# An attention step that begins with a pair of scores and maxima, and orders the two halves of its background by a one-column read

## The chip, the core and the metric

The kernel runs on one core of a Trainium2 chip. The metric is the device time of one execution in microseconds; lower is better.

The engines of the core, with the names that the profile gives them: TensorE (PE, matmuls; PEld, the loading of a matmul's weights, which overlaps the matmul before), VectorE (DVE), ScalarE (ACT), GpSimd (POOL), and the queue that issues DMAs (SP). Matmul results go to eight banks of PSUM, each 128 x 512 numbers of 32 bits.

## The reference

A transformer block with a conditioning vector: layer norm, attention with 32 heads of 16 dimensions over 2048 tokens of width 512, and a feed-forward part of width 1792.

```python
mod = (silu(c) @ w_mod).reshape(1, 6, 1, 512)
sa, ca, ga, sb, cb, gb = (mod[:, i] for i in range(6))
h = layernorm(x) * (1 + ca) + sa
q, k, v = heads(h @ wqkv)                       # 32 heads, 16 dimensions each
p = softmax(q @ k.T * 16 ** -0.5)               # 2048 x 2048 for each head
x = x + ga * ((p @ v) @ wo)
h = layernorm(x) * (1 + cb) + sb
x = x + gb * (gelu(h @ w1 + b1) @ w2 + b2)
```

## The kernel before

After a prologue of some 110 us the kernel walks through attention in 512 **steps** (`half_step(hs)`, `for hs in range(NU * NKC)`): 32 units of one block of 512 queries and a group of four heads, times 16 blocks of 128 keys. All else that TensorE has to do (projections, output projection, both feed-forward products) is put between the attention matmuls as **background**. At the end a tail of some 120 us does the last block's feed-forward part.

Four kinds of matmul stand in a step:

- `mx` (`mx_mm`, L387): scores of a unit that comes later, only to find their maxima. VectorE reduces each to one column, negated (`reduce`, L392). The maxima are sent through DRAM into two more rows of the queries, so that the scores of the unit come out with their maximum taken off.
- `e` (`exp_mm`, L637): the scores themselves. ScalarE turns each into a tile `p` by an exponential (L642).
- `bg` (`bg_mm`, through `mm`, L274): background.
- `pv` (`pv_step`, L667): four matmuls with `p`, one for each head of the group, at the step's end.

`e`, `mx` and `bg` use only 64 rows of the array (50, 48 and 64 of them), so two run at once, one in each **half** of the rows. A step of number `hs` has half `h = hs % 2`: six background matmuls go to half `h`, and `e` and `mx` beside them to the other half, `1 - h`. Two matmuls beside each other are called a **pair** here. A step has seven: six with background and one of an `e` in half `h` and an `mx` in half `1 - h`. So each step has four `e`, four `mx`, six `bg` and the four `pv`; with the background of two steps both halves of the rows have added to the result.

A group of background (12 or 18 terms for each half) takes four or six steps, and all its matmuls add to one bank. At its end ScalarE, by `evac`, copies the bank out (`y` L834 and L906, `h` L880, `pf` L308, `vr` L322).

Matmuls of the two halves that add to one bank may not run at once. So where a group goes on in the other half, its first matmul there waits for an instruction of ScalarE that can only be done after the last matmul of the half before: `saw` notes the first such instruction after each background matmul, and `bg_mm` adds the dependency.

```python
        if g["n"] and g["half"] != h:
            tc.add_manual_dep(ins, g["seen"].name, AFTER, reason="both halves of the rows add to one bank")
        g["half"], g["seen"] = h, None
```

Banks go round in rings: three for `e` (0, 1, 2), three for `mx` (3, 4, 5), one for `pv` (6), one for `bg` (7). A matmul into a bank waits until the bank's last reader is done, so the fourth `e` of a step waits for the exponential of the first, and an `mx` for the reduction of the third `mx` before it. Each engine works off its instructions in the order in which the program writes them.

Some steps differ: 12 in which `turn_v` first transposes values on TensorE and ScalarE copies them (`vst`, L338), 12 that begin with the transposes of a layer norm's result (`h`, L853), 13 in which no background is ready, and the last 22, for which no maxima are left. ScalarE also does the Tanh of the feed-forward part (`s`, L886), copies weights (`wqkv`, L190) and takes each unit's result out of its bank (`osb`, L654). VectorE finds each unit's minimum of the negated maxima (`mn`, L404), transposes it (`mt`, L406), and does statistics of rows (`bst`, `mv`, `rt`) and reciprocals (`dn`).

Of the kernel before, what the change touches and what calls it, by code (L numbers as in the profile page):

```python
# [8 lines left out]
F32 = mybir.dt.float32  # L9
FR = mybir.dt.float32r  # L10
AF = mybir.ActivationFunctionType
# [5 lines left out]
P = 128  # L17
# [42 lines left out]
RUN = 6  # L60
# [9 lines left out]
def block_kernel(ctx: ExitStack, tc: tile.TileContext, x, wqkv, wo, w1, b1, w2, b2, c, w_mod, out):  # L70
    nc = tc.nc
    te, ve, ac, gp, sy = nc.tensor, nc.vector, nc.scalar, nc.gpsimd, nc.sync
# [13 lines left out]
    def bank(i, name):  # L86
        return bank_pools[i].tile([P, TB], F32, tag=f"bank{i}", name=name)
# [6 lines left out]
    def take(name):  # L94
        ids = rings[name]
        turn[name] += 1
        return bank(ids[(turn[name] - 1) % len(ids)], name)
# [13 lines left out]
    const = ctx.enter_context(tc.tile_pool(name="const", bufs=1))  # L111
# [12 lines left out]
    gb_b = const.tile([P, D], F32, name="gb_b")  # L124
    b2_b = const.tile([P, D], F32, name="b2_b")
    b1_h = const.tile([P, NF], F32, name="b1_h")


    kqcm, kqpool = pool("kq")
# [27 lines left out]
    first = [True]  # L157
# [109 lines left out]
    def advance():  # L267
        clock["t"] += 1
        for f in hooks.pop(clock["t"], []):
            f()  # L270
# [82 lines left out]
    def kh(u, h):  # L353
        return khalf[(2 * u + h) % 5]

    def load_rows(dst, w, g, t0, t1):

        ap = qk_d[w][g // 2].rearrange("i d (g p a) t -> g a (i d) p t", g=2, p=2)
        for a in range(2):
            sy.dma_start(dst[a * 64 : a * 64 + KR].bitcast(F32), ap[g % 2, a, :, :, t0:t1])  # L360
# [5 lines left out]
    def load_q(u):  # L366
# [2 lines left out]
        qst[u] = kqpool.tile([P, 2, TB], FR, tag="qst", name="qst", bufs=3)  # L369
        load_rows(qst[u], 0, g, qb * TB, (qb + 1) * TB)  # L370

    xc, red, mrows = [0, 0], {}, set()
    xorder = [int(t[1]) for t in SCRIPT.split() if t[:2] in ("X0", "X1") for _ in range(int(t[3:] or 1))]
    xorder = [(u, xorder[:n].count(u)) for n, u in enumerate(xorder)]
# [2 lines left out]
    def mx_mm(a):  # L377

        u, i = xorder[xc[a]] if xc[a] < 64 else divmod(xc[a], 32)
        xc[a] += 1  # L380
        kr, p, qc = i // 8, (i // 4) % 2, i % 4
        if u not in mxp:
            mxp[u] = small.tile([P, 16, 4], F32, tag="mxp", name="mxp")
            red[u] = 0
        ps = take("mx")
        r0 = a * 64
        te.matmul(ps, qst[u][r0 : r0 + KR, p, qc * P : (qc + 1) * P],  # L387
                  kh(u, kr // 2)[r0 : r0 + KR, p, (kr % 2) * TB : (kr % 2 + 1) * TB], start=True, stop=True)
        hc = (a * 2 + p) * 4 + qc

        def reduce():
            ins = ve.tensor_reduce(mxp[u][:, hc, kr : kr + 1], ps, axis=AX.X, op=ALU.max, negate=True)  # L392
            red[u] += 1
            if red[u] == 64:
                max_rows(u)
            return ins

        return reduce
# [3 lines left out]
    def max_rows(u):  # L402
        m = mn[u % 2]
        ve.tensor_reduce(m[:, :16], mxp.pop(u), axis=AX.X, op=ALU.min)  # L404
        mt = small.tile([P, 32], F32, tag="mt", name="mt")
        ve.transpose(mt, m)  # L406
        m2 = small.tile([P, 2, 32], FR, tag="m2", name="m2")
        gp.tensor_copy(m2[:, 0], mt)
        gp.tensor_tensor(m2[:, 1], mt, m2[:, 0].bitcast(F32), op=ALU.subtract)

        def store():
            for i in range(2):
                sy.dma_start(m_d[u][i].rearrange("x b j -> b x j"), m2[:, i].bitcast(F32))

        def load():
            mrows.add(u)
            for a in range(2):
                r0 = a * 64 + KR
                sy.dma_start(qst[u][r0 : r0 + 2].bitcast(F32).rearrange("s p t -> s (p t)"),
                             m_d[u][:, a * 8 : a * 8 + 8].rearrange("s x b j -> s (x b j)"))  # L420

        if u:
            later(5, store)
            later(11, load)
        else:
            rows.update(store=store, load=load)
# [142 lines left out]
    for token in SCRIPT.split():  # L569
        name, ids, e, n = re.fullmatch(r"([A-Za-z]+)(\d*)(?:\.([avg]))?(?:\*(\d+))?", token).groups()  # L570
# [52 lines left out]
    ec, begun = [0, 0], [0]  # L623
    cur = {"pv": 0}

    def exp_mm(a, bk="e"):

        s, p = divmod(ec[a], 2)
        while begun[0] < min(ec) // 2 + 1:
            begun[0] += 1  # L630
            step_start(begun[0] - 1)
        ec[a] += 1
        u, kc = divmod(s, NKC)
        assert u in mrows, (u, ec, xc, red, clock["t"])
        r0 = a * 64
        ps = take(bk)
        te.matmul(ps, kh(u, kc // 8)[r0 : r0 + KX, p, (kc % 8) * P : (kc % 8 + 1) * P], qst[u][r0 : r0 + KX, p],  # L637
                  start=True, stop=True)

        def act():  # L640
            t = ppool.tile([P, TB], F32, tag="p", name="p")
            saw(ac.activation(t, ps, AF.Exp, scale=SCALE))  # L642
            pt[4 * s + p * 2 + a] = t
            advance()

        return act
# [122 lines left out]
    def wload():  # L769

        n = len(wt)
        if n == len(stream) or "f" not in pools:
            return
        key = stream[n]
        if extra:
            t = extra.pop()
        elif len(ringed) < WB or ringed[-WB] in used:
            t = pools["f"].tile([P, 2, D], FR, tag="w", name=f"w{key[1]}", bufs=WB)
            ringed.append(key)
        else:  # L780
            return
        sy.dma_start(t.bitcast(F32), {"o": wo_d, 1: w1_d, 2: w2_d}[key[1]][key[2]])
        wt[key] = t
# [198 lines left out]
    act = {"g": None}  # L982

    def saw(ins):

        if act["g"] and not act["g"]["seen"]:
            act["g"]["seen"] = ins.ins
# [23 lines left out]
    def half_step(hs):  # L1011
        h = hs % 2
        if h or len(wt) < len(used) + KC:
            wload()
        if sides:
            sides.pop(0)()
        full = False
        if act["g"] is None:
            j = held.pop() if held else next(jobs, None)
            if callable(j):  # L1020
                j()
                full = True
                j = next(jobs, None)
            if callable(j):
                held.append(j)
            elif j is not None:
                act["g"] = {"group": j, "at": [0, 0], "n": 0, "seen": None}
        nx = min(64 * NU, LEAD + 4 * (hs + 1))
        ne = 4 * (hs + 1)

        def x_ok(a):
            return sum(xc) < nx and xc[a] < 32 * NU

        def e_ok(a):
            return sum(ec) < ne and ec[a] < 2 * NU * NKC

        more = act["g"] is not None
        free = not more and not full
        k = 0
        while more and k < RUN:  # L1040
            a = 1 - h
            more = bg_mm(h)
            if e_ok(a) and (sum(ec) < ne - 1 and k % 2 == 1 or not x_ok(a) and (sum(ec) < ne - 1 or k == RUN - 1)):
                exp_mm(a)()
            elif x_ok(a):
                mx_mm(a)()
            k += 1
        while sum(ec) < ne or sum(xc) < nx:
            a = 0 if ec[0] <= ec[1] else 1
            fs = []  # L1050
            if sum(ec) < ne:
                fs.append(exp_mm(a, "bg" if free and sum(ec) == ne - 1 else "e"))
                if x_ok(1 - a):
                    fs.append(mx_mm(1 - a))
                elif e_ok(1 - a):
                    fs.append(exp_mm(1 - a))
            else:
                fs += [mx_mm(i) for i in range(2) if x_ok(i)]
            for f in fs:
                f()  # L1060
        if hs:
            assert min(ec) >= 2 * cur["pv"] + 2
            pv_step()
# [5 lines left out]
    def step_start(s):  # L1069
        u, kc = divmod(s, NKC)  # L1070
        for d in [d for d in due if d[0] <= s and all(k in stored for k in d[1])]:
            due.remove(d)
            d[2]()
        if kc == 0 and u + 2 < NU:
            g = (u + 2) % NG // 2
            due.append((16 * u + 6, [(0, g, (u + 2) // NG)], lambda: load_q(u + 2)))
            for b, n in enumerate((6, 8, 12, 13)):
                t0 = b % 2 * TB
                due.append((16 * u + n, [(1, g, b)], lambda b=b, t0=t0: load_k(u + 2, b // 2, t0, t0 + TB)))
        if kc == 0 and u + 1 < NU:  # L1080
            for h in range(2):
                need = [(2, (u + 1) % NG // 2, b) for b in (2 * h, 2 * h + 1)]
                due.append((16 * u + 11 + h, need, lambda h=h: load_v(u + 1, h)))
        if preps and s % 3 == 2:
            prep(*preps.pop(0))
        try_prep()

    for hs in range(NU * NKC):
        half_step(hs)
# [137 lines left out]
```

## Time and profile before

| what | value |
|---|---|
| median of three runs | 1730.08 us (1729.0 to 1730.61) |
| the profiled execution, first to last instruction | 1728.4 us |
| TensorE, matmuls | 1699.9 us busy, 98% of the span |
| VectorE | 1375.0 us, 80% |
| ScalarE | 1246.1 us, 72% |
| GpSimd | 694.7 us, 40% |
| mean granted TensorE clock | 0.999 of full speed |

The page gives the profiled execution no time of its own beside its span, which stands 1.7 us below the median. A row of a timeline gives start, length, engine, line, operation, output and inputs, and in brackets how long the engine was idle before and what ended that. Rows that follow each other and are alike are joined (x4). A row of a group has the busy time, the mean length of one in ns, and the idle time before. A row of the waits has who waited, for whom, us in total, times, and the longest. A row of a window has its bounds, its length, and busy time and count of PE and PEld; the last three numbers are the granted clock, the DMA engines' busy share and GB/s.

### The profile page before, as it was taken

To read this page: it belongs to the slowest core of one execution; us is meant where nothing else is said; L and a number is where in the kernel's file an instruction comes from. 1 tells how busy PE (TensorE), PEld (TensorE's weight loads), DVE (VectorE), ACT (ScalarE), POOL (GpSimd) and SP (SyncE) were. 2 spreads that over 40 slices of the span, in tenths; PEclk is the share of its full clock that TensorE was granted. 3 is DMA by queue.
4 is the path that set the end of the run, shared out by engine and by line. 5 is a ranking of instruction groups with operands and counts; after the bars stand their busy time and mean duration, and the time that the engine had idled before them with its cause. 6 is when DMAs were issued, how large, how long until landed. Compare 5 with 4: busy or idle time off the path is not lost.

```text
span 1728.4 us, 32510 instructions
## 1 busy us (share of the span) xinstructions
PE 1699.9 (98%) x12133; PEld 890.7 (52%) x12133; DVE 1375.0 (80%) x2307; ACT 1246.1 (72%) x2379; POOL 694.7 (40%) x703
## 2 busy tenths in 40 slices
PE   7999999999999999999999999999999999999999
PEld 5654444444444444444445444444445444444777
DVE  7998888888888888888889888888889888860332
ACT  3357778778777788778877788778877788778231
POOL 7333534435121457306623246306633256326310
PEclk9999999999999999999999999999999999999999
DMA  8746776767447534325453443345463354423444
GB/s 291 219 137 199 220 219 183 236 180 221 125 139 209 126 98 114 94 77 154 116 161 94 125 119 108 94 107 154 108 179 79 109 133 112 106 80 99 184 158 164
DMA packets 137129, 251.89 MB, mean 146 GB/s; under 512 B 25854, under 2 KB 45324, under 8 KB 136972
## 3 DMA queue, kind: packets, MB, share of 16 engines
q1 hardware_dynamic: 135712, 248.19, 50.3%
q8 instruction: 96, 1.57, 0.4%
q10 hardware_dynamic: 1260, 1.63, 0.3%
q14 instruction: 61, 0.50, 0.1%
HBM read 188.49 MB, written 61.28 MB: 145 GB/s over the span
## 4 chain that ended last, share of the span: by engine, by line
PE 91%; DVE 3%; DMA 2%; ACT 2%; POOL 1%; issue 1%; SPq 0%; ACTq 0%; DVEq 0%; POOLq 0%
PE bg L274 46%; PE pv L667 29%; PE e L637 11%; PE mx L387 3%; DVE mxp L392 2%; PE pr L274 1%; ACT p L642 1%; PE o L274 1%; DMA wm<-in_w_mod_dram 0%; DMA wt<-wos 0%; ACT h L853 0%; PE mx L333 0%; PE bg L851 0%; DMA rden<-dn 0%; DVE bst L235 0%
## 5 line engine op out<-in xcount | busy, mean ns | idle before, releaser
L392 DVE TENSOR_REDUCE mxp<-mx 128x1 f32<-128x512 f32 x2048 | 1269.6, 681 | 192.8 <-PE mx L387 160.6
L642 ACT ACTIVATE p<-e 128x512 f32<-128x512 f32 x2035 | 1072.9, 604 | 296.7 <-PE e L637 285.7
L387 PE MATMUL mx<-kh,qst 48*128 48x512 f32 x2048 | 865.3, 436 | 1.4 <-DVE mxp L392 0.3
L637 PE MATMUL e<-qst,kh 50*128 50x512 f32 x2035 | 747.6, 414 | 6.6 <-ACT p L642 6.4
L667 PE MATMUL pv<-p,vg 128*32 128x512 f32 x4096 | 546.1, 605 | 0.0
L637 PEld LDWEIGHTS e<-qst,kh 50*128 50x128 f32 x2035 | 374.2, 186 | 135.7 <-ACT p L642 128.5
L387 PEld LDWEIGHTS mx<-kh,qst 48*128 48x128 f32 x2048 | 369.0, 185 | 21.6 <-DVE mxp L392 14.9
L274 PE MATMUL bg<-w,g 64*128 64x512 f32 (+1 forms) x1056 | 280.6, 404 | 0.0
L274 PEld LDWEIGHTS bg<-w,g 64*128 64x128 f32 (+1 forms) x1056 | 185.3, 185 | 142.7 <-ACT p L642 83.9
L274 PE MATMUL bg<-pchi,w 64*128 64x512 f32 (+1 forms) x664 | 197.5, 417 | 2.3 <-ACT p L642 2.2
L274 PEld LDWEIGHTS bg<-pchi,w 64*128 64x128 f32 (+1 forms) x664 | 110.1, 184 | 153.2 <-ACT p L642 103.3
L274 PE MATMUL bg<-hThi,wqkv 64*128 64x512 f32 x560 | 167.4, 418 | 0.3 <-ACT p L642 0.3
L274 PEld LDWEIGHTS bg<-hThi,wqkv 64*128 64x128 f32 x560 | 92.8, 184 | 118.8 <-ACT p L642 106.3
L667 PEld LDWEIGHTS pv<-p,vg 128*32 128x32 f32 x4096 | 81.2, 108 | 124.6 <-issue 120.5
L888 POOL TENSOR_SCALAR s<-s 128x512 f32<-128x512 f32 x41 | 61.4, 1498 | 120.5 <-ACT s L886 120.5
L907 POOL TENSOR_TENSOR x<-y,x 128x512 f32<-128x512 f32 x28 | 36.0, 1287 | 153.5 <-ACT y L906 153.5
L274 PE MATMUL bg<-pclo,w 64*128 64x512 f32 (+1 forms) x332 | 90.1, 390 | 0.0
L876 DVE TENSOR_TENSOR g<-h,g 128x512 fp32r<-128x512 f32 x15 | 10.9, 725 | 88.1 <-ACT g L875 88.1
L274 PE MATMUL bg<-hTlo,wqkv 64*128 64x512 f32 x280 | 76.4, 391 | 0.0
L274 PEld LDWEIGHTS bg<-pclo,w 64*128 64x128 f32 (+1 forms) x332 | 61.2, 184 | 12.2
L274 PE MATMUL bg<-wo,pchi 64*128 64x512 f32 x192 | 64.6, 416 | 0.0
L881 POOL TENSOR_TENSOR s<-h 128x512 f32<-128x512 f32 x41 | 42.7, 1042 | 47.7 <-ACT h L880 47.6
(158 smaller groups left out, 1299.1 us busy)
## 6 DMA issues: line engine op xcount, KB each, us to landing
kh<-qk SPq DMA_DIRECT2D x256, 192.0 KB
w<-w1s SPq DMA_DIRECT2D x56, 512.0 KB
w<-w2s SPq DMA_DIRECT2D x54, 512.0 KB
vg<-v SPq DMA_DIRECT2D x64, 332.0 KB
qk<-parts SPq DMA_DIRECT2D x32, 512.0 KB
qst<-qk SPq DMA_DIRECT2D x64, 192.0 KB
qk<-parts SPq DMA_DIRECT2D x32, 256.0 KB
ou<-osb SPq DMA_DIRECT2D x32, 256.0 KB
```

The source lines that it names most:

```text
L274: return te.matmul(ps, term[0][r], term[1][r], start=i == 0, stop=i == n - 1)
L387: te.matmul(ps, qst[u][r0 : r0 + KR, p, qc * P : (qc + 1) * P], kh(u, kr // 2)[r0 : r0 + KR, p, (kr % 2) * TB : (kr % 2 + 1) * TB], start= ...
L392: ins = ve.tensor_reduce(mxp[u][:, hc, kr : kr + 1], ps, axis=AX.X, op=ALU.max, negate=True)
L637: te.matmul(ps, kh(u, kc // 8)[r0 : r0 + KX, p, (kc % 8) * P : (kc % 8 + 1) * P], qst[u][r0 : r0 + KX, p], start=True, stop=True)
L642: saw(ac.activation(t, ps, AF.Exp, scale=SCALE))
L667: te.matmul(cur["ps"][32 * j : 32 * (j + 1)], vg[u][:, kc, j * VW : j * VW + 32], pt.pop(4 * s + j), start=kc == 0, stop=kc == NKC - 1)
L876: ve.tensor_tensor(g[:, 1], h, g[:, 0].bitcast(F32), op=ALU.subtract)
L881: gp.tensor_tensor(s, h, h, op=ALU.mult)
L888: gp.tensor_scalar(s, s, 1.0, None, op0=ALU.add)
L907: later(4, lambda: gp.tensor_tensor(x2[t], y, x2[t], op=ALU.add))
```

## The change

A step that has background begins with the pair of `e` and `mx` that stood at its end. Six pairs with background follow, in which the other three `e` stand at the first, third and fifth place and the other three `mx` at the second, fourth and sixth (before, `mx` came first). Since no `e` follows the last background matmul now, ScalarE gets a new instruction where the group goes on: a copy of one column of the last `mx` bank into a tile `tick` that nobody reads. The next step's first background matmul depends on it. Steps without background or without maxima left are written as before.

```diff
+    tick = const.tile([P, 1], F32, name="tick")
...
+    mxb = [None]
...
-        ps = take("mx")
+        mxb[0] = ps = take("mx")
...
         more = act["g"] is not None
         free = not more and not full
         k = 0
+        first = more and x_ok(1 - h) and e_ok(h)
+        if first:
+            for f in [exp_mm(h), mx_mm(1 - h)]:
+                f()
         while more and k < RUN:
             a = 1 - h
             more = bg_mm(h)
-            if e_ok(a) and (sum(ec) < ne - 1 and k % 2 == 1 or not x_ok(a) and (sum(ec) < ne - 1 or k == RUN - 1)):
+            if first:
+                if e_ok(a) and (k % 2 == 0 if x_ok(a) else sum(ec) < ne - 1 or k == RUN - 1):
+                    exp_mm(a)()
+                elif x_ok(a):
+                    mx_mm(a)()
+            elif e_ok(a) and (sum(ec) < ne - 1 and k % 2 == 1 or not x_ok(a) and (sum(ec) < ne - 1 or k == RUN - 1)):
                 exp_mm(a)()
             elif x_ok(a):
                 mx_mm(a)()
             k += 1
+        if first and more and not act["g"]["seen"]:
+            saw(ac.activation(tick, mxb[0][:, :1], AF.Copy))
```

Lines after the first hunk move down by one or two, so L387, L392, L637, L642 and L667 are L389, L394, L639, L644 and L669 in the changed kernel; `tick` is L1060. In its order there are 354 ticks and 450 steps with seven pairs.

On TensorE, before, around the end of a step and the start of the next, beside background of the feed-forward part (`pchi` its input, `w` a weight, `kh` keys, `qst` queries; in brackets the semaphores that an instruction waits for, named by the engine or the DMA queue that raises them, Activation being ScalarE):

```order
L637 MATMUL e<-qst,kh_193 128x512 [waits Activation_49]
L274 MATMUL bg<-pchi_5322,w_11064 128x512
L387 MATMUL mx<-kh_191,qst 128x512 [waits DMAHW4_49,DVE_49]
L274 MATMUL bg<-pchi_5322,w_11064 128x512
L637 MATMUL e<-qst,kh_193 128x512 [waits Activation_49] x2
L387 MATMUL mx<-kh_191,qst 128x512 [waits DVE_49]
L667 MATMUL pv<-p,vg 32x512 x4
L274 MATMUL bg<-pchi_5322,w_11064 128x512 [waits Activation_49]
L387 MATMUL mx<-kh_191,qst 128x512 [waits DVE_49]
```

The third `e` goes with the sixth background matmul, the fourth `e` and the fourth `mx` make the last pair, and the next step's first background matmul comes right after `pv`.

On TensorE, after the change, at a like place (end of a step, start of the next):

```order
L275 MATMUL bg<-pchi_5392,w_10047 128x512
L639 MATMUL e<-qst,kh_193 128x512 [waits Activation_49]
L275 MATMUL bg<-pchi_5392,w_10047 128x512
L389 MATMUL mx<-kh_191,qst 128x512 [waits DVE_49]
L669 MATMUL pv<-p,vg 32x512 [waits PE_49]
L669 MATMUL pv<-p,vg 32x512 x3
L639 MATMUL e<-qst,kh_193 128x512 [waits Activation_49]
L389 MATMUL mx<-kh_190,qst 128x512 [waits DVE_49]
L275 MATMUL bg<-pchi_5392,w_10047 128x512 [waits Activation_49]
L639 MATMUL e<-qst,kh_193 128x512
```

The fourth `e` has moved from the last pair to the last but one, background stands in the last, and the pair of `e` and `mx` stands between `pv` and the first background matmul, which still waits for ScalarE.

On ScalarE, after the change, the end of one step and the next three, the middle one of which ends a group (`h` is its evacuation):

```order
L1060 ACTIVATE tick<-mx 128x1 [waits DVE_49,Activation_49]
L644 ACTIVATE p<-e 128x512 [waits PE_49] x4
L1060 ACTIVATE tick<-mx 128x1 [waits DVE_49,Activation_49]
L644 ACTIVATE p<-e 128x512 [waits PE_49] x4
L882 ACTIVATE h<-bg,b_h 128x512 [waits PE_49]
L644 ACTIVATE p<-e 128x512 [waits PE_49] x2
L644 ACTIVATE p<-e 128x512 [waits PE_49,Activation_49]
L644 ACTIVATE p<-e 128x512 [waits PE_49]
L1060 ACTIVATE tick<-mx 128x1 [waits DVE_49,Activation_49]
```

Before, a step's four exponentials had nothing of this kind behind them, and `h` stood between the second and the third. The tick waits for VectorE, not for TensorE: the count for which it waits is that of the reduction of the same `mx` bank, the step's fourth.

## The prediction

> **What bounds the kernel now.** First the page's busy time and chain, to find the engine that sets the end; then the groups, for the durations of what the change touches; then the waits.
>
> ```profile
> PE 1699.9 (98%) x12133; PEld 890.7 (52%) x12133; DVE 1375.0 (80%) x2307; ACT 1246.1 (72%) x2379; POOL 694.7 (40%) x703
> PE 91%; DVE 3%; DMA 2%; ACT 2%; POOL 1%; issue 1%; SPq 0%; ACTq 0%; DVEq 0%; POOLq 0%
> L392 DVE TENSOR_REDUCE mxp<-mx 128x1 f32<-128x512 f32 x2048 | 1269.6, 681 | 192.8 <-PE mx L387 160.6
> PEld e L637 <- ACT p L642: 128.5, 483, 1.1
> ```
>
> TensorE carries 91% of the chain, so what counts is the length of one attention step on it. The last line is the wait that the new order might spare: 483 times a score's weights wait for an exponential, 0.27 us each. How much of that is on the path shows in one step, here the weight loads (start, length, what).
>
> ```profile
> 894.00 0.18 PEld L274 LDWEIGHTS bg<-wo,pchi 64*128 64x128 f32 x1 [0.84 <-ACT p L642]
> 894.11 0.19 PEld L637 LDWEIGHTS e<-qst,kh 50*128 50x128 f32 x1
> 894.34 0.18 PEld L274 LDWEIGHTS bg<-wo,pclo 64*128 64x128 f32 x1
> ...
> 895.06 0.19 PEld L637 LDWEIGHTS e<-qst,kh 50*128 50x128 f32 x1
> 895.49 0.18 PEld L637 LDWEIGHTS e<-qst,kh 50*128 50x128 f32 x1 [0.24 <-ACT p L642]
> 895.49 0.18 PEld L387 LDWEIGHTS mx<-kh,qst 48*128 48x128 f32 x1
> 895.92 0.16 PEld L667 LDWEIGHTS pv<-p,vg 128*32 128x32 f32 x8 [0.25 <-issue]
> 896.92 0.18 PEld L274 LDWEIGHTS bg<-wo,pchi 64*128 64x128 f32 x1 [0.84 <-issue]
> ```
>
> Seven pairs, then `pv`, in 2.92 us. The first pair's weights are loaded in the open, so the second pair's follow after 0.11; from there a pair takes 0.23, the load hidden under the pair before. The seventh pair's loads should stand at 0.11 + 5 x 0.23 = 1.27 after the start, and stand at 1.49: the fourth score takes the bank of the first (the ring has three), and that one's exponential is read out until 1.44. `pv` follows 0.43 later and takes 1.00.
>
> What six pairs cost when nothing waits is shown by the one step that has background alone, from its first load, in the open, to `pv` (1.60) and to the next step (2.59):
>
> ```profile
> 1603.98 0.29 PEld L274 LDWEIGHTS bg<-pchi,w 64*128 64x128 f32 x2 [0.84 <-ACT p L642]
> 1605.58 0.16 PEld L667 LDWEIGHTS pv<-p,vg 128*32 128x32 f32 x8 [0.36 <-issue]
> 1606.57 0.53 PEld L274 LDWEIGHTS bg<-pchi,w 128*128 128x128 f32 x3 [0.84 <-issue]
> ```
>
> A seventh pair adds 0.23: 2.82 is the floor of a step, and 2.92 is now 0.10 above it. ScalarE and VectorE in the same step:
>
> ```profile
> 894.84 0.60 ACT L642 ACTIVATE p<-e 128x512 f32<-128x512 f32 x1 [0.85 <-PE e L637]
> 894.84 2.06 ACT L642 ACTIVATE p<-e 128x512 f32<-128x512 f32 x4 [0.85 <-PE e L637]
> 894.57 2.48 DVE L392 TENSOR_REDUCE mxp<-mx 128x1 f32<-128x512 f32 x4 [0.43 <-PE mx L387]
> 897.48 2.48 DVE L392 TENSOR_REDUCE mxp<-mx 128x1 f32<-128x512 f32 x4 [0.43 <-PE mx L387]
> ```
>
> Four exponentials from 0.84 to 2.90, one each 0.49; the first ends at 895.44 and the load it holds back starts at 895.49, so a handover to TensorE takes 0.05. Four reductions run without a gap, 0.60 apart, from 0.57 to 3.05: **the fourth ends 0.13 after the next step has begun**. Nothing in the kernel before waits for it there. The mean step comes from `pv` loads (eight records a step) between the first and the last full steps:
>
> ```profile
> 112.10:1538.90 1426.80, 518.90 (x3900) 76.69 (x3896) 1.00 0.50 138
> ```
>
> 3896 / 8 = 487 steps in 1426.8 us. In the order, 450 of them have seven pairs; 24 begin with four transposes and 13 have no background. The two kinds are read from these rows (3.50 and 2.74 us); the loads of the second begin with a score beside a maximum, as every step will after the change:
>
> ```profile
> 157.01 0.42 PEld L333 LDWEIGHTS mx<-ident,vr 128*128 128x128 f32 x4 [0.84 <-DVE mxp L392]
> 159.09 0.18 PEld L637 LDWEIGHTS e<-qst,kh 50*128 50x128 f32 x1 [0.25 <-ACT p L642]
> 160.51 0.18 PEld L274 LDWEIGHTS bg<-hThi,wqkv 64*128 64x128 f32 x1 [0.84 <-ACT p L642]
> ...
> 527.13 0.18 PEld L637 LDWEIGHTS e<-qst,kh 50*128 50x128 f32 x1 [0.84 <-ACT p L642]
> 527.67 1.57 ACT L642 ACTIVATE p<-e 128x512 f32<-128x512 f32 x3 [0.67 <-PE mx L387]
> 529.87 0.18 PEld L637 LDWEIGHTS e<-qst,kh 50*128 50x128 f32 x1 [0.84 <-ACT p L642]
> ```
>
> (1426.8 - 24 x 3.50 - 13 x 2.74) / 450 = **2.904 us** for an ordinary step.
>
> **The change, part by part.** *The order of the pairs.* TensorE issues the same 14 matmuls and `pv`; nothing is added there. The exponentials start earlier: a score in the first pair is in ScalarE after 0.54 (527.13 to 527.67). But the fourth score moves forward by a pair too, from the seventh to the sixth. It can load at 0.54 + 0.60 + 0.05 = 1.19, against 0.11 + 4 x 0.23 = 1.03 wanted; its matmul then begins 0.11 later, at 1.30, where unhindered it would at 1.27. So 0.03 of wait is left where 0.10 was: steps of 2.85. Alone this is worth 450 x (2.904 - 2.85) = -24 us.
>
> *The one-column read (tick).* Every maximum stays in pairs 1, 3, 5 and 7, so the reductions stay from 0.57 to 3.05 after the start. In the order all 354 ticks wait for VectorE's semaphore, at the count of the reduction that reads the same bank, the fourth; and the next step's first background matmul waits for the tick. Behind it, in TensorE's queue, stand that step's second score, its maxima and `pv`. No row shows a tick; the nearest are ScalarE's two narrowest reads, 14 columns from PSUM and 4 from SBUF.
>
> ```profile
> 22.05 0.17 ACT L563 ACTIVATE b_h<-pr 128x14 f32<-128x14 f32 x1
> 2.91 0.20 ACT L216 ACTIVATE s_c<-c_c 128x4 f32<-128x4 f32 x1 [0.91 <-DMA c_c<-in_c_dram]
> ```
>
> I take 0.17, since it reads PSUM too; the other end is 0.20, and without any cost of its own it would be 0. For the handover VectorE to ScalarE I take the 0.05 that ScalarE to TensorE shows, between 0 and 0.2. The second pair can then load at b = 3.05 + 0.05 + 0.17 + 0.05 - L = 3.32 - L after the start of its step, L being the length of the step before. From b there are six pairs, the first in the open, and `pv`: 2.60 (2.59 above, rounded up). So the next step is 5.92 - L long: two steps in a row make 5.92, a mean of **2.96**. Steps of 2.85 would leave b at 0.47, 0.36 later than 0.11; a longer step waits less for its own tick, and this is where it settles. A group of background ends in every fourth or sixth step; there its evacuation (0.59 to 0.69 us) stands behind the fourth exponential instead of the tick: 0.54 + 4 x 0.49 = 2.50, ready at 3.10 to 3.20, the next pair at 0.24 or less, which the 0.03 and the open load absorb. The step after such a short one pays its rest back. Sum: 450 x (2.96 - 2.904) = **+25 us**; with a tick and handovers of 0.2 in all +10, with 0.2 more than taken +70.
>
> The Trainium skill, "ScalarE: Activation LUTs", section "What ACT_TABLE_LOAD costs", gives an activation 186 ns plus 0.83 per column. By it a tick is about 0.19, an estimate, and the sum +29.
>
> *VectorE's other work.* What stands among a step's reductions delayed none of TensorE's next loads, or by 0.1 us; now it delays the tick, and so the step, in full.
>
> ```profile
> 888.50 0.22 DVE L404 TENSOR_REDUCE mn<-mxp 128x16 f32<-128x64 f32 x1
> 888.96 2.44 DVE L392 TENSOR_REDUCE mxp<-mx 128x1 f32<-128x512 f32 x4
> ...
> 905.05 0.68 DVE L235 BATCH_NORM_STATS2 bst<-x 128x6 f32<-128x512 f32 x1
> 905.77 0.18 DVE L236 BATCH_NORM_AGGREGATE mv<-bst 128x2 f32<-128x6 f32 x1
> 905.87 1.85 DVE L392 TENSOR_REDUCE mxp<-mx 128x1 f32<-128x512 f32 x3
> 907.64 0.14 DVE L826 TENSOR_SCALAR rt<-mv 128x1 f32<-128x1 f32 x1
> 907.70 1.28 DVE L392 TENSOR_REDUCE mxp<-mx 128x1 f32<-128x512 f32 x2
> ...
> L715 DVE RECIPROCAL dn<-dn 128x32 f32<-128x32 f32 x16 | 5.5, 342 | 9.1 <-DMA dn<-ou 9.1
> ```
>
> In the order these stand ahead of a tick: a unit's minimum and transpose 8 times (888.50 to 888.96: 0.46), row statistics 11 times (0.82 + 0.06), a reciprocal 11 times (0.3). 3.7 + 9.7 + 3.3 = **+16 us**; as little as 0 if the slack of other waits takes them.
>
> *ScalarE's queue.* The 12 steps with value transposes have the first exponential held back by the copies, so the fourth score's load (159.09, 2.08 after the start) stays where it is, and one pair more now follows it: 12 x 0.23 = +3. The ten weight casts of 0.98 us that stood behind the fourth exponential stand ahead of a tick, which the casts delay by some 0.2 to 0.3: +2. Tanh stands after the second exponential now; the tick still has the reduction to wait for, so nothing. POOL and SP get the same instructions, DMAs too, within half a step of where they were.
>
> Sum: 25 + 16 + 3 + 2 = +46 on the profiled 1728.4 us; I round down to +44, as a few of the waits now in the mean of 2.904 go. 1772 in the profile, **1774** for the median of runs, which stands 1.7 above the profiled span. The range goes from half of the first two terms (20 + 5, 1755) to 0.05 more in the handovers, counted in full (+22, 1796).
>
> **The rivals.** *Faster:* the tick is hidden, and all 450 steps take 2.85: -24 + 5, 1711. It decides at b below 0.25, that is, a tick that ends by 3.05, when the reduction ends. For it: ScalarE is idle by then (0.85 before each batch). Against: the wait in the order; only a fourth reduction some 0.27 earlier would do. The Trainium skill, "PSUM — Partial Sum Buffer", section "Terms", has two engines on one bank at a time as an error, reads against reads included; by that rule the wait can't be a scheduler's chance, and I give this 0.05.
>
> *No change:* tick and both handovers together 0.16 instead of 0.27, so two steps make 5.81 and the mean is 2.905, with VectorE's other work lost in slack: 1732. Chance 0.05.
>
> *Much slower:* above b = 0.37 the second maximum comes later than its reduction's slot (a hidden load is read 0.69 later; b + 0.11 + 0.69 against 0.57 + 0.60), and a further delay moves the reductions as well, so it counts in full and not by half. b settles at 0.36, at this edge. 0.1 more in the handovers would then be 450 x 0.1 = +45: 1819. Chance 0.10.
>
> **How the numbers follow.** Forecast 0.80, faster 0.05, no change 0.05, much slower 0.10. Faster or slower counts from 0.2% (3.5 us), about what a measurement of this kernel can tell from no change; the second rival lies within it. So faster 0.05, same 0.05, slower 0.80 + 0.10. The range of 1755 to 1796 leaves out the three rivals, 2 in 10.
>
> **What would show it.** After: the first exponential 0.54 after a step's start; the fourth score's wait much shorter than 0.27; ticks of about 0.17 right behind the fourth reduction; a wait of the second pair's background for the tick, some 0.25 us, some 350 times; steps of 2.85 after a group's end, of 2.93 to 3.06 elsewhere. It would be wrong if the ticks start before the fourth reduction ends, or if the reductions begin earlier than 0.57.

## The result, and the profile after

The changed kernel takes 1796.3 us (1795.1 to 1797.12, four runs) against 1729.73 us (1729.0 to 1730.61): a ratio of 1.0382, 95% interval 1.0369 to 1.0395. It is **66.6 us slower**, where +44 was forecast. The range's upper end was 1796; the median stands 0.3 above it, less than the runs of this kernel lie apart. The profiled execution has a span of 1795.3 us, 66.9 more than before.

From the page of the changed kernel, the busy times, the chain and the group of the tick:

```profile
PE 1749.1 (97%) x12133; PEld 904.0 (50%) x12133; DVE 1397.9 (78%) x2307; ACT 1305.0 (73%) x2733; POOL 695.2 (39%) x703
PE 82%; DVE 9%; ACT 4%; DMA 2%; issue 1%; POOL 1%; SPq 0%; ACTq 0%; DVEq 0%; POOLq 0%
L1060 ACT ACTIVATE tick<-mx 128x1 f32<-128x1 f32 x354 | 60.9, 172 | 193.1 <-DVE mxp L394 190.4
```

TensorE issues as many matmuls as before, but its share of the chain falls from 91% to 82%, and what it loses stands with VectorE (3% to 9%) and ScalarE (2% to 4%). The tick takes 172 ns, as assumed; before it ScalarE waits for VectorE's reductions. The waits say the same from both sides:

```profile
ACT tick L1060 <- DVE mxp L394: 190.4, 310, 1.8
PEld bg L275 <- ACT tick L1060: 100.6, 327, 1.4
```

TensorE's weight loads wait 327 times for a tick, 0.31 us each; none of this stood in the kernel before. The tick also reads a bank of the `mx` ring, but no `mx` waits for a tick in this trace. The `pv` instructions from the first to the last full step, as a row of windows:

```profile
115.46:1603.77 1488.31, 518.93 (x3900) 76.68 (x3896) 17.95 (x30) 1.00 0.48 132
```

The same 487 steps take 1488.3 us instead of 1426.8: 61.5 of the 66.9 lie here. The other 5.4 lie before and behind: the first full step begins at 115.5 instead of 112.1, and behind the last come 191.5 instead of 189.5. About 1.0 of this falls in the first two steps and in the step behind the last one counted, which have the new order too; the other 4.4 lie where the code is the same. With the prediction's formula an ordinary step is now (1488.3 - 24 x 3.50 - 13 x 2.74) / 450 = 3.041 us. One settled step on PEld, ACT and DVE:

```profile
888.45 0.18 PEld L639 LDWEIGHTS e<-qst,kh 50*128 50x128 f32 x1 [0.84 <-issue]
888.84 0.18 PEld L275 LDWEIGHTS bg<-w,g 64*128 64x128 f32 x1 [0.21 <-ACT tick L1060]
...
889.65 0.19 PEld L639 LDWEIGHTS e<-qst,kh 50*128 50x128 f32 x1
889.86 0.18 PEld L275 LDWEIGHTS bg<-w,g 64*128 64x128 f32 x1
...
891.44 0.18 PEld L639 LDWEIGHTS e<-qst,kh 50*128 50x128 f32 x1 [0.84 <-ACT p L644]
891.84 0.18 PEld L275 LDWEIGHTS bg<-w,g 64*128 64x128 f32 x1 [0.21 <-ACT tick L1060]
```

```profile
888.98 2.07 ACT L644 ACTIVATE p<-e 128x512 f32<-128x512 f32 x4 [0.19 <-PE mx L389]
891.62 0.17 ACT L1060 ACTIVATE tick<-mx 128x1 f32<-128x1 f32 x1 [0.56 <-DVE mxp L394]
```

```profile
889.02 2.50 DVE L394 TENSOR_REDUCE mxp<-mx 128x1 f32<-128x512 f32 x4 [0.49 <-PE mx L389]
```

The step runs from 888.45 to 891.44, 2.99 us. The first exponential comes 0.53 after its start, and the fourth score's load at 889.65 stands in line with its neighbours and waits for nothing. The fourth reduction ends at 889.02 + 2.50 = 891.52. The tick starts at 891.62, 0.10 later, and ends at 891.79; the background's load follows at 891.84, which is b = 0.40. From there the step takes 2.60. So the chain is the one forecast, but the first handover is 0.10 where 0.05 was taken. A step behind a group's end has no tick to wait for and is short, here 885.11 - 882.27 = 2.84:

```profile
882.27 0.18 PEld L639 LDWEIGHTS e<-qst,kh 50*128 50x128 f32 x1 [0.84 <-issue]
885.11 0.18 PEld L639 LDWEIGHTS e<-qst,kh 50*128 50x128 f32 x1 [0.84 <-ACT p L644]
```

### The profile page after: what moved, and what is told of

It is laid out like the page before. It is cut to its first block, busy times and chain, and to the rows that moved or that the text cites. A ratio compares the mean times of both kernels' runs of the same rounds, so it can differ in the third digit from the quotient of the medians.

```text
span 1795.3 us, 32900 instructions
## 1 busy us (share of the span) xinstructions
PE 1749.1 (97%) x12133; PEld 904.0 (50%) x12133; DVE 1397.9 (78%) x2307; ACT 1305.0 (73%) x2733; POOL 695.2 (39%) x703
## 4 chain that ended last, share of the span: by engine, by line
PE 82%; DVE 9%; ACT 4%; DMA 2%; issue 1%; POOL 1%; SPq 0%; ACTq 0%; DVEq 0%; POOLq 0%
PE bg L275 38%; PE pv L669 25%; PE e L639 13%; DVE mxp L394 7%; PE mx L389 3%; ACT p L644 2%; PE pr L275 1%; DMA w<-w1s 1%; DVE bst L236 1%; PE o L275 1%; DMA wm<-in_w_mod_dram 0%; ACT h L855 0%; DMA wt<-wos 0%; DVE hTlo L483 0%; ACT tick L1060 0%
## 5 line engine op out<-in xcount | busy, mean ns | idle before, releaser
L394 DVE TENSOR_REDUCE mxp<-mx 128x1 f32<-128x512 f32 x2048 | 1291.4, 684 | 235.2 <-PE mx L389 197.2
L644 ACT ACTIVATE p<-e 128x512 f32<-128x512 f32 x2035 | 1068.2, 602 | 111.5 <-PE mx L389 75.5
L639 PE MATMUL e<-qst,kh 50*128 50x512 f32 x2035 | 844.4, 441 | 6.2 <-ACT p L644 6.2
L389 PE MATMUL mx<-kh,qst 48*128 48x512 f32 x2048 | 834.7, 422 | 2.3 <-DVE rt L828 0.6
L639 PEld LDWEIGHTS e<-qst,kh 50*128 50x128 f32 x2035 | 367.9, 185 | 411.7 <-ACT p L644 218.3
L669 PE MATMUL pv<-p,vg 128*32 128x512 f32 x4096 | 545.6, 605 | 0.0
L389 PEld LDWEIGHTS mx<-kh,qst 48*128 48x128 f32 x2048 | 370.1, 185 | 20.7 <-DVE mxp L394 14.1
L1060 ACT ACTIVATE tick<-mx 128x1 f32<-128x1 f32 x354 | 60.9, 172 | 193.1 <-DVE mxp L394 190.4
L275 PE MATMUL bg<-pchi,w 64*128 64x512 f32 (+1 forms) x664 | 193.3, 410 | 6.0 <-ACT tick L1060 2.5
L669 PEld LDWEIGHTS pv<-p,vg 128*32 128x32 f32 x4096 | 80.6, 108 | 178.8 <-issue 168.1
L275 PE MATMUL bg<-hThi,wqkv 64*128 64x512 f32 x560 | 162.8, 410 | 3.8 <-ACT tick L1060 2.7
L275 PEld LDWEIGHTS bg<-hThi,wqkv 64*128 64x128 f32 x560 | 96.4, 185 | 38.0 <-ACT tick L1060 28.0
```

What stands on the lines that cost most here:

```text
L275: return te.matmul(ps, term[0][r], term[1][r], start=i == 0, stop=i == n - 1)
L669: te.matmul(cur["ps"][32 * j : 32 * (j + 1)], vg[u][:, kc, j * VW : j * VW + 32], pt.pop(4 * s + j), start=kc == 0, stop=kc == NKC - 1)
L1060: saw(ac.activation(tick, mxb[0][:, :1], AF.Copy))
```

## The experiments

All are edits of the changed kernel, unless something else is said. The theory: TensorE waits for VectorE's fourth reduction by way of ScalarE, and that alone costs the time. The rivals: the new order of pairs costs it, or the ticks' time on ScalarE. Counts and means over the 450 ordinary steps (the steps with seven pairs) are read from the weight loads in a run's trace.

**The same tick at the same place, without VectorE.**

```diff
-            saw(ac.activation(tick, mxb[0][:, :1], AF.Copy))
+            t = ac.activation(tick, mhalf[:, :1], AF.Copy)
+            tc.add_manual_dep(t.ins, act["g"]["last"].name, AFTER, reason="the half is done")
+            saw(t)
```

`g["last"]` is the latest background matmul.

> The order of pairs, the tick, its place in ScalarE's queue and what waits for it stay as in the changed kernel; but the tick copies a column of a constant and waits for the last background matmul instead of reading the bank that VectorE reduces. Theory (the wait for VectorE's fourth reduction costs the time, the order is a gain): the tick stands behind the fourth exponential, 0.54 + 4 x 0.49 = 2.50, done at 2.67, released at 2.72, before the next step begins at 2.85; no wait, VectorE's other work hidden again; steps of 2.85 instead of 3.04, 450 x 0.19 = -85: 1711. Rival 1 (the new order itself costs, or the tick's time on ScalarE): stays at 1780 to 1800. Rival 2 (the order gains nothing): steps of 2.90, 1732.

Measured: 1728.75 us, ratio to the kernel before 0.9984 (0.9976 to 0.9993). The order, the 354 ticks and TensorE's wait for them are all still there, and 67.5 us are gone: the loss hangs on the tick's wait for VectorE. It is not the tick's time on ScalarE by itself, for this tick is longer (225 ns against 172). Settled steps are 2.83 to 2.85 as expected, but the time is not 1711; it is the one that rival 2 gave, and only the steps tell the two apart. The row of windows gives a mean of (1423.3 - 119.6) / 450 = 2.897:

```profile
112.36:1535.68 1423.32, 518.90 (x3900) 76.67 (x3896) 17.96 (x30) 1.00 0.50 138
```

Where the rest went is seen on ScalarE, and then on PEld, in the step from 831.15 and the next:

```profile
831.68 1.09 ACT L643 ACTIVATE p<-e 128x512 f32<-128x512 f32 x2 [0.69 <-PE mx L388]
832.65 0.63 ACT L887 ACTIVATE s<-s 128x512 f32<-128x512 f32 x1
833.17 1.09 ACT L643 ACTIVATE p<-e 128x512 f32<-128x512 f32 x2
834.13 0.22 ACT L1059 ACTIVATE tick<-mhalf 128x1 f32<-128x1 f32 x1
```

```profile
833.98 0.18 PEld L638 LDWEIGHTS e<-qst,kh 50*128 50x128 f32 x1 [0.84 <-ACT p L643]
...
834.40 0.18 PEld L275 LDWEIGHTS bg<-pchi,w 64*128 64x128 f32 x1 [0.24 <-ACT tick L1059]
```

A Tanh among the exponentials pushes the tick to 834.13, past the next step's start at 833.98, and the background waits 0.3 longer than the 0.11 of a step without a wait. Weight casts and evacuations do the same: in 138 of the 450 ordinary steps the first background load stands later than 0.15.

**The tick and the evacuation ahead of the fourth exponential**, with the tick of the last experiment.

```diff
-                    exp_mm(a)()
+                    hold.append(exp_mm(a))
+                    if k < RUN - 2:
+                        hold.pop()()
...
+        for f in hold:
+            f()
```

The first lines hold the last exponential back; the loop stands behind the tick.

> As the tick on the last background matmul, but the tick and the evacuation at a group's end are written ahead of the step's fourth exponential on ScalarE. With the tick behind it, the trace showed settled steps of 2.84, and 99 steps above 2.90: background waited where a Tanh (36 steps, 6.2 us in all), a weight cast (10 steps, 5.3) or an evacuation (93 steps, 5.4) had pushed the tick or the evacuation past the next step's start. Theory (ScalarE's queue ate the order's gain of 24 us): the tick runs from 2.0 to 2.23 and the evacuation from 2.0 to 2.65, and these waits go, -17 of 1729: 1709 to 1715. Rival 1 (the delayed fourth exponential, then done at 2.85 to 3.25, holds up a later bank or ScalarE as a whole): 1725 to 1740. Rival 2 (the rest is something else): 1729.

Measured: 1715.9 us, ratio 0.9919 (0.9904 to 0.9934), 0.9 above the expected range. It is 0.8% below the kernel before and 4.5% below the changed one. One row of windows, and the like place on ScalarE:

```profile
114.09:1524.41 1410.32, 518.88 (x3900) 76.66 (x3896) 18.14 (x30) 1.00 0.51 140
```

```profile
827.61 0.62 ACT L887 ACTIVATE s<-s 128x512 f32<-128x512 f32 x1
828.13 1.08 ACT L643 ACTIVATE p<-e 128x512 f32<-128x512 f32 x2
829.09 0.21 ACT L1061 ACTIVATE tick<-mhalf 128x1 f32<-128x1 f32 x1
829.18 0.61 ACT L643 ACTIVATE p<-e 128x512 f32<-128x512 f32 x1
```

Beside a Tanh the tick now ends at 829.30, before the next step starts (829.43), and in all 450 ordinary steps the first background load stands at 0.11. Mean step (1410.3 - 119.6) / 450 = 2.868: 0.029 less than with the tick behind the exponential, 13 us. Against the kernel before, most of the order's gain is there once ScalarE's queue lets it through.

**The reduction itself orders**, no tick.

```diff
-            saw(ac.activation(tick, mxb[0][:, :1], AF.Copy))
+            saw(mxb[0])
```

Here `mxb[0]` holds the instruction of the latest reduction.

> No tick: the next step's first background matmul waits for the fourth reduction itself. Theory: ScalarE's hop (0.09 + 0.17 + 0.05) becomes one handover from VectorE to TensorE (0.05 to 0.09), so b = 3.05 + 0.05 to 0.09 - L, two steps 5.70 to 5.74, steps of 2.85 to 2.87; VectorE's other work still delays the wait (+5 to +16): 1716 to 1736. Rival (the wait for the reduction costs, whatever stands behind it): 1780 to 1796. Rival (steps of 2.90 are the order's own): 1735 to 1750.

Measured: 1739.54 us, ratio 1.0051 (1.0037 to 1.0064), 3.5 above the expected range. Without ScalarE's hop 56.8 us are gone although TensorE still waits for the reduction. So the wait for the reduction alone costs little; what stands behind it in the changed kernel, some 0.3 us of handover, tick and handover, reaches past the cover of the first pair. A step's and the next one's first load, the background's between them, and the reductions that it waits for:

```profile
870.66 0.18 PEld L638 LDWEIGHTS e<-qst,kh 50*128 50x128 f32 x1 [0.84 <-issue]
...
870.94 0.18 PEld L274 LDWEIGHTS bg<-w,g 64*128 64x128 f32 x1
...
873.53 0.18 PEld L638 LDWEIGHTS e<-qst,kh 50*128 50x128 f32 x1 [0.84 <-ACT p L643]
```

```profile
868.40 2.49 DVE L393 TENSOR_REDUCE mxp<-mx 128x1 f32<-128x512 f32 x4 [0.47 <-PE e L638]
```

The fourth reduction ends at 870.89, the load follows at 870.94, b is 0.28 and the step 2.87. The 10.8 us over the tick on the matmul lie where VectorE does other work: the 63 ordinary steps that have some of it from 0.5 after the start of the step before to 0.5 after their own take 3.15 on average, where the 62 like ones with the tick on the matmul take 2.96; the others take 2.88 in both.

**Two ticks**, one behind the other.

```diff
+            ac.activation(tick, mxb[0][:, :1], AF.Copy)
             saw(ac.activation(tick, mxb[0][:, :1], AF.Copy))
```

> Two ticks, one behind the other, both reading the bank of the last maximum; the second one orders. The second adds some 0.17 to b. If a delay counts by half (two steps have a fixed sum): 354 x 0.085 = +30, 1826. If it counts in full (the reductions move with the delayed background): 354 x 0.17 = +60, 1856. Rival (the tick is hidden and the order or VectorE's extra work costs): 1796.

Measured: 1861.68 us, ratio 1.0758 (1.0743 to 1.0772), +65.4 over the changed kernel. Two rows of ScalarE and the load that waits:

```profile
923.63 0.17 ACT L1060 ACTIVATE tick<-mx 128x1 f32<-128x1 f32 x1 [0.66 <-DVE mxp L394]
923.84 0.17 ACT L1061 ACTIVATE tick<-mx 128x1 f32<-128x1 f32 x1
```

```profile
920.25 0.18 PEld L639 LDWEIGHTS e<-qst,kh 50*128 50x128 f32 x1 [0.84 <-issue]
920.85 0.18 PEld L275 LDWEIGHTS bg<-w,g 64*128 64x128 f32 x1 [0.42 <-ACT tick L1061]
...
923.45 0.18 PEld L639 LDWEIGHTS e<-qst,kh 50*128 50x128 f32 x1 [0.84 <-ACT p L644]
```

The second tick ends 0.21 after the first, b is 0.60, the step 3.20: 0.21 longer than 2.99. A delay counts nearly in full here, 65.4 of at most 354 x 0.21 = 74, and not by half; the time is 5.7 above the 1856 of "in full" because the second tick adds 0.21 and not 0.17. The reductions show why; in this step they take 2.72 from first to last where 2.50 was enough, since the second maximum waits with the background ahead of it; in the trace the second reduction starts 0.83 after the first, in the changed kernel 0.61:

```profile
920.82 2.72 DVE L394 TENSOR_REDUCE mxp<-mx 128x1 f32<-128x512 f32 x4 [0.48 <-PE mx L389]
```

**Ticks into 32 columns in turn.**

```diff
-            saw(ac.activation(tick, mxb[0][:, :1], AF.Copy))
+            ticks[0] += 1
+            saw(ac.activation(tick[:, ticks[0] % 32 : ticks[0] % 32 + 1], mxb[0][:, :1], AF.Copy))
```

In the order a tick then waits for one semaphore instead of two, VectorE's; that for ScalarE's own last tick, long done, is gone.

> The changed kernel, but each tick writes another of 32 columns, so that it waits for VectorE alone and no longer for ScalarE's own last tick as well. In the trace of after the ticks start 0.09 to 0.10 behind the fourth reduction, where 0.05 was taken. If the second wait makes the other 0.04: 354 x 0.04 = -14, 1782. If VectorE's handover to ScalarE takes 0.09 by itself: unchanged, 1794 to 1798.

Measured: 1778.53 us, ratio 1.0279 (1.0264 to 1.0294): 17.8 us less. A step's first load, the reductions' row and the tick's:

```profile
880.03 0.18 PEld L639 LDWEIGHTS e<-qst,kh 50*128 50x128 f32 x1 [0.84 <-issue]
```

```profile
880.60 2.48 DVE L394 TENSOR_REDUCE mxp<-mx 128x1 f32<-128x512 f32 x4 [0.49 <-PE mx L389]
```

```profile
883.12 0.17 ACT L1061 ACTIVATE tick<-mx 128x1 f32<-128x1 f32 x1 [0.49 <-DVE mxp L394]
```

The reduction ends at 883.08 and the tick starts at 883.12: 0.04 instead of 0.10, the rest of the kernel being the same; 0.09 was expected to become 0.05, so 17.8 us came where 14 were worked out. Where the 0.06 lie is seen in the changed kernel's trace. One row of a query about the tick's line (count, then ns as least, median and greatest, then the first and last start, and a count by shape in a sample; ACTq is ScalarE's sequencer, which is not counted as busy):

```profile
L1060 ACTq EVENT_SEMAPHORE  x347: 17/17/17, 115.6 to 1603.9; - x174
```

Of the 354 ticks 347 have such an instruction ahead of them. It carries the wait for VectorE, and the tick itself that for ScalarE. In the step shown there it starts at 891.55, 0.03 behind the reduction, and the tick 0.06 after it. With ticks in columns no tick has one. The second wait made the difference, and its 354 x 0.06 = 21 us come back at 0.8 of their size.

**No statistics of rows beside attention.**

```diff
-            ln_stat(mv, t, x2[t])
+            gp.memset(mv[:, t], 1.0)
```

> The changed kernel without the 12 statistics of rows that VectorE works out beside attention (bst and mv; mean and variance are set to 1 by GpSimd instead, so the feed-forward part gets wrong numbers; the timing of the rest stays). Theory (VectorE's other work delays the tick in full): 11 steps that were 0.7 to 1.2 us longer become ordinary ones: -8 to -12, 1784 to 1788. Rival (lost in slack): 1796.

Measured: 1787.62 us, ratio 1.0331 (1.0316 to 1.0347), 8.7 us less than the changed kernel; 7.2 of them lie between the first and the last full step (1481.1 instead of 1488.3). In that kernel a step with them on VectorE before its fourth reduction held the tick back like this, then TensorE:

```profile
573.78 0.17 ACT L1060 ACTIVATE tick<-mx 128x1 f32<-128x1 f32 x1 [1.32 <-DVE mxp L394]
```

```profile
572.92 0.18 PEld L639 LDWEIGHTS e<-qst,kh 50*128 50x128 f32 x1 [0.84 <-issue]
574.00 0.18 PEld L275 LDWEIGHTS bg<-wo,pchi 64*128 64x128 f32 x1 [0.90 <-ACT tick L1060]
```

The background stands at 1.08 after the step's start instead of 0.40: some 0.7 in this one, at the lower end of the 0.7 to 1.2 expected.

**The old order with a tick**, an edit of the kernel before: the tick is written at the end of the step, behind its last pair.

```diff
+        if first and more:
+            act["g"]["seen"] = ac.activation(tick, mxb[0][:, :1], AF.Copy).ins
```

> The order of pairs as before the change; only the tick is added at each step's end where the group goes on, and the next step's first background matmul waits for it instead of an exponential. Theory: no pair stands ahead of the waiting background matmul, so the whole step starts late: the fourth reduction ends 3.05 after a step's start, plus 0.09 + 0.17 + 0.05 gives steps of 3.36 instead of 2.90 where a group goes on, 354 x 0.46 = +163, less what the group's ends win: 1870 to 1900. Rival 1 (the order is what costs, the tick is cheap): 1735 to 1750. Rival 2 (the tick costs what the changed kernel lost against steps of 2.85, +85): 1815.

Measured: 1918.24 us, ratio 1.1084 (1.1067 to 1.1101), 18 above the expected range. From PEld, DVE and ACT:

```profile
946.13 0.18 PEld L275 LDWEIGHTS bg<-w,g 64*128 64x128 f32 x1 [1.56 <-ACT tick L1065]
949.50 0.18 PEld L275 LDWEIGHTS bg<-w,g 64*128 64x128 f32 x1 [1.35 <-ACT tick L1065]
```

```profile
946.70 2.48 DVE L394 TENSOR_REDUCE mxp<-mx 128x1 f32<-128x512 f32 x4 [0.89 <-PE mx L389]
```

```profile
949.27 0.17 ACT L1065 ACTIVATE tick<-mx 128x1 f32<-128x1 f32 x1 [0.27 <-DVE mxp L394]
```

A settled step is 949.50 - 946.13 = 3.37, where 3.36 was worked out. The expectation had left out VectorE's other work, which the prediction put at 16 for the changed kernel; that this makes up the 18 was not tried. With background at a step's head the tick costs 187 us over the kernel before. In the changed kernel, where a pair that needs no tick stands at the head, the tick and the new order together cost 67. So the new order covers part of the tick's wait and is not the loss.

**The scores behind the maxima**, so that the fourth exponential orders and no tick is needed.

```diff
-                if e_ok(a) and (k % 2 == 0 if x_ok(a) else sum(ec) < ne - 1 or k == RUN - 1):
+                if e_ok(a) and (k % 2 == 1 if x_ok(a) else sum(ec) < ne - 1 or k == RUN - 1):
```

> The step still begins with the pair of a score and a maximum, but the other scores stand at the second, fourth and sixth place of the background pairs and the maxima at the first, third and fifth, so that the fourth exponential orders the halves and no tick is needed. Theory: the fourth maximum, now in the sixth pair, waits for the bank of the first, released at 1.25 + 0.05, where 1.03 was wanted; its matmul begins at 1.41 at the latest where 1.27 was wanted: steps of 2.84 to 2.96, 1715 to 1755, most likely 1740; VectorE's other work delays it too. Rival (an exponential behind the last background pair costs like the tick, since it ends after the next step's start): 1780 or more.

Measured: 1768.02 us, ratio 1.0217 (1.0199 to 1.0234), above the expected range.

```profile
874.09 0.18 PEld L639 LDWEIGHTS e<-qst,kh 50*128 50x128 f32 x1 [0.84 <-issue]
...
875.40 0.18 PEld L389 LDWEIGHTS mx<-kh,qst 48*128 48x128 f32 x1
875.41 0.18 PEld L275 LDWEIGHTS bg<-w,g 64*128 64x128 f32 x1
875.51 0.19 PEld L639 LDWEIGHTS e<-qst,kh 50*128 50x128 f32 x1
876.07 0.16 PEld L669 LDWEIGHTS pv<-p,vg 128*32 128x32 f32 x8 [0.37 <-issue]
877.07 0.18 PEld L639 LDWEIGHTS e<-qst,kh 50*128 50x128 f32 x1 [0.84 <-ACT p L644]
```

No background waits at the head of this step, so the rival is not what happens here; but the fourth maximum's load comes at 1.31, with the bank of the first, and so the step is 2.98, as 438 of the 450 ordinary steps are to within 0.03. Against 2.904 that alone is some 34 of the 38 us. The cause was expected; the upper end of what it gives, 2.96 a step, was a little short. This order is no way around the tick.

## Why the prediction was right, and what was mis-sized

Direction, place and mechanism held: the first exponential at 0.53 (0.54 forecast), no wait left before the fourth score, ticks of 0.17 behind the fourth reduction, the second pair's background waiting 327 times (some 350 forecast) for 0.31 (0.25), steps of 2.84 after a group's end. By its own terms:

- *The handover from VectorE to ScalarE*, taken as 0.05 "between 0 and 0.2", is the mis-sized term. It measured 0.10. The order had shown the cause: the tick waits for two semaphores. With the reductions ending at 3.07 the two steps' sum is 5.99 instead of 5.92, a settled step 3.00 instead of 2.96: 450 x 0.035 = 16 us. That two steps have a fixed sum is seen at the groups' ends: the short step of 2.84 is followed by one of 3.13 (median of 90), 5.97 together; the 2.93 to 3.06 that were forecast for all other steps left these long ones out. With one wait less (0.04) the mean step was (1471.3 - 119.6) / 450 = 3.004, from this row of the kernel with ticks in columns; the prediction's terms give 2.96 + 18 / 450 = 3.00.

```profile
114.88:1586.22 1471.34, 518.91 (x3900) 76.71 (x3896) 17.95 (x30) 1.00 0.48 134
```

- *By half or in full.* The fourth reduction was taken to end 3.05 after a step's start whatever b is. It does so up to b of about 0.35 (ticks in columns: 880.60 + 2.48 - 880.03). At b = 0.40 it ends at 3.07, and with two ticks, at b = 0.60, at 920.82 + 2.72 - 920.25 = 3.29. So a delay comes through at 0.8 of its size between the ticks in columns and the changed kernel, and at 65 of 74 beyond: the mechanism of the rival "much slower", which set its edge at b = 0.37. The changed kernel stands just behind that edge.
- *The order of the pairs, -24.* This is no term of the sum; the rival "faster" rests on it. Without VectorE in the chain the order gave 450 x (2.904 - 2.897) = -3; with ScalarE's queue put right 450 x (2.904 - 2.868) = -16; where the other 8 are was not tried. What the term missed is ScalarE: "Tanh stands after the second exponential now; ... so nothing" is true only as long as the tick waits for the reduction anyway. In the changed kernel it does, and this hid the error.
- *VectorE's other work, +16.* (Its three parts add up to 16.7.) The statistics, the largest part (9.7), measured 8.7, and 7.2 within the steps; the reciprocals and minima weren't tried apart.
- *Value transposes, +3.* It didn't come: in such steps of the changed kernel the fourth score's load stood 1.89 after the start, not at 2.08, and they are 0.03 longer.
- The rival "faster" needed a tick that ends by 3.05. The tick on the matmul does, and came to 1728.75, not 1711, for the reason under the order of the pairs; with that put right it was 1715.9.

In all 46 was worked out and 66.9 measured on the span: some 18 for the ordinary steps, -3 for the transposes, and 5 outside the full steps, where the first of them begins at 112.1 in the kernel before and at 112.4 to 115.5 in the nine others; all but 1.0 of that part is not explained. The range's upper end was worked out from what happened, 0.05 more in the handovers counted in full; that the time met it this closely is luck all the same, as the 5 and the -3 are in it.

## What to carry to other kernels

When an instruction is added only to order others, look at what it waits for, not at what it costs: a one-column read of 0.17 us cost 67 us because it could start only when its bank had been reduced, and the way back from it then reached past the next step's first pair; a copy of a column of a constant, tied to the matmul that it has to follow, left the time where it was before the change. Then look at its place in its own queue: ahead of the last long instruction instead of behind it was worth another 13 us. And count the semaphores that it waits for: each tick here paid 0.06 for a second one that had long been raised.

## What the runs showed of the hardware

- An instruction of ScalarE that waits for two semaphores, one of them long raised, started 0.10 after the reduction it waited for; with one it started 0.04 after. The Trainium skill, "Perfetto Trace Analysis", section "Identifying Dependency Chains", says that instructions which wait on several engines may get further instructions ahead of them to carry the additional waits; the trace agrees, with 347 of 354 ticks behind such an instruction in the changed kernel and none in the one with ticks in columns. The page gives no price; 0.06 is what these traces show.
- A one-column copy took 172 ns from PSUM, by the group of the changed kernel, and 225 from SBUF, by that of the tick on the matmul:

```profile
L1059 ACT ACTIVATE tick<-mhalf 128x1 f32<-128x1 f32 x354 | 79.7, 225 | 0.0
```

The same page, section "Optimizing Scalar/DVE Operations", puts ScalarE's overhead at some 93 ns on SBUF and 51 on PSUM, as busy time, and says that the profiled latency is about twice that: a difference of 42, or 84 by an estimate from the doubling. The 225 - 172 = 53 agree in sign but are not that difference alone, since all 354 copies from SBUF began while the instruction ahead of them still ran. With the tick ahead of the fourth exponential, three copies from SBUF began on an idle ScalarE and took 0.20, 0.03 more than from PSUM.
